# First loads as float32 on hardware queues, and batch 0's swapped x normed from its raw copy

## The chip, the cores and the metric

The kernel runs on one core of a Trainium2 chip. The metric is the device time of a whole execution in microseconds (us). A profile is one of these executions; its span is some 2 us shorter than the time. The profile calls the engines PE (TensorE), PEld (its weight loads), DVE (VectorE), ACT (ScalarE), POOL (GpSimd) and SP (SyncE).

## The reference, cut to what matters

```python
# 8 batches, 12 heads, 448 positions, head size 64
scores = scale * q @ k.T
attn = np.maximum(scores, 0.0) ** 2 / S
x = (attn @ v) in token order            # 3584 tokens, 768 features
rms = np.sqrt(np.mean(x * x, axis=-1, keepdims=True) + 1e-06)
xn = x / rms * rms_g
g = xn @ w_gate ; val = xn @ w_val       # 768 -> 1536
out = (silu(g) * val) @ w_out            # 1536 -> 768
```

## The kernel before: the parts that matter

The kernel handles one batch after the other. While PE multiplies batch b by the gate and value weights, pieces of the attention of batch b+1 are woven in. Batch 0 has no predecessor: its attention runs first, with nothing to hide behind. Three things are needed for what follows.

First, the loads. All of q, k and v come through the software queue (issued by POOL), which casts float32 to bf16 on the way:

```python
load("q", 0, 0, 2);  load("k", 0, 0, 2)      # first pair of heads
... # identity, constants, warm-up tile
load("q", 0, 2, 6);  load("k", 0, 2, 6)      # four heads in one load
load("v", 0, 0, 6)
load("q", 0, 6, 12); load("k", 0, 6, 12); load("v", 0, 6, 12)
for s in range(2): fetch_gv(s)               # first slices of the weights
alloc_ld(1)                                  # then q and k of batch 1, halves
```

Second, two layouts of x. A gate block multiplies 64 rows of x by gate weights and the other 64 rows by value weights at the same time, so each x is kept twice: `xT`, and `xD` with its two halves of 64 partitions swapped. `xD` is made by DMA (`swap`):

```python
def swap(b, j0, j1, eng=None):
    for hf in (0, 1):
        (eng or nc.sync).dma_start(out=xDs[b][own half, j0:j1, :], in_=xTs[b][other half, j0:j1, :])
```

Third, the order after the attention of batch 0. Three early blocks (`psE`) use the raw, not yet normed x and are scaled later; from the fourth block on (`psG`, `psV`) the normed x is used:

```python
rounds(0, 0, blocks[0], 0, KT, raw_x)      # early block 0, half that needs xT
norm_stat(0)                               # sums of squares on PE, root on ACT, reciprocal on DVE
rounds(0, 1, blocks[1], 0, KT, raw_x)
... # early blocks: first the part of raw xD that has landed
norm_apply(0)                              # six products on DVE into a new xT, swapped into a new xD by DMA
... # rest of raw xD, early block 2, then blocks 3 to 11 with normed xT and xD
```

`warm(n)` puts n dummy matmuls (`psW`) on PE to keep its clock up.

## Time and profile before

| | before |
|---|---|
| time, median of 4 fast runs | 463.41 us (463.32 to 463.87) |
| span of the profiled run | 461.8 us |
| PE busy | 97% |
| from 68 to 100 us, PE busy | 30.73 of 32 us |

PE is the bound from about 64 us on. What can be won lies before that. The lines below are from the page of the kernel before: busy time by engine, and the granted TensorE clock in 40 slices of the span, in tenths of full speed.

```profile
span 461.8 us, 10803 instructions
PE 445.7 (97%) x4718; PEld 249.4 (54%) x4718; DVE 268.2 (58%) x318; ACT 284.8 (62%) x425; POOL 53.6 (12%) x79
PEclk9799899999999999999999999999999999999999
```

Next, the table by stretches of the kernel before. The columns are: stretch; its length; busy us and instructions of PE, PEld, DVE, ACT and POOL; granted clock; mean DMA occupation; GB/s.

```profile
6.00:8.00 2.00, 0.55 (x4) 0.11 (x4) 0.42 (x1) 1.12 (x2) 2.00 (x4) 1.00 1.38 181
8.00:10.00 2.00, 0.56 (x17) 0.48 (x18) 0.00 (x0) 0.60 (x1) 2.00 (x4) 1.00 1.22 159
12.00:14.00 2.00, 2.00 (x16) 0.70 (x15) 2.00 (x3) 1.59 (x2) 0.70 (x1) 0.50 1.33 172
44.00:48.00 4.00, 3.95 (x26) 1.97 (x27) 3.24 (x6) 2.22 (x4) 0.70 (x1) 0.66 1.51 195
```

PE is hardly busy from 6 to 10 us, and then runs at half clock until 18 us (0.50 in the three stretches from 12 to 18); a second half-clock time falls into 44 to 49 us. The timeline of PE shows the waits; in brackets stands the idle time just before, and what ended it.

```profile
9.44 0.39 PE L134 MATMUL psT<-ident,kb 112*64 112x112 bf16 x8 [2.42 <-DMA kb<-in_k_dram]
36.08 1.42 PE L447 MATMUL psE<-xT,wgv_sb 64*128 64x448 bf16 x12
42.98 0.35 PE L447 MATMUL psE<-xD,wgv_sb 64*128 64x448 bf16 x1 [0.64 <-DMA xD<-xT]
44.02 0.72 PE L447 MATMUL psE<-xD,wgv_sb 64*128 64x448 bf16 x5 [0.69 <-DMA xD<-xT]
53.24 0.35 PE L447 MATMUL psG<-xD,wgv_sb 64*128 64x448 bf16 x1
54.14 0.35 PE L447 MATMUL psV<-xD,wgv_sb 64*128 64x448 bf16 x1 [0.56 <-DMA xD<-xT]
62.82 1.71 PE L263 MATMUL psAV<-r,vb 112*64 112x448 bf16 x16
```

The first wait is for K of the second head pair, the next two for the raw swaps, the fourth for the swap of the normed x. And this is the chain that ended last in the same kernel (start, us, what), from the statistics on:

```profile
37.49 1.27 PE psSS L380 x12
38.79 0.64 ACT rstd L389
39.45 2.96 DVE rstd L393
42.44 3.31 DVE xT L427 x6
46.28 7.82 DMA xD<-xT
54.14 0.35 PE psV L447
```

The chain does not run through PE's raw-swap waits or its half clock between 42 and 49 us at all: it runs through the norm and its swap. (0.9 us is the distance of the two starts at 53.24 and 54.14: a `psG` and a `psV` matmul run as a pair elsewhere, and here the second one came late. PE stood wholly idle for 0.56 us of it.)

### The profile page before, as it was taken

The page shows a single profiled execution, that of the slowest core. Times are in us where ns is not written, and L with a number is a line of the kernel's source. Part 1 is how long each engine was busy: PE and PEld are TensorE (multiplying, and loading weights), DVE is VectorE, ACT ScalarE, POOL GpSimd, SP SyncE. Part 2 cuts the span into 40 slices and gives each one's busy share as a digit, 9 for nine tenths or more (in the row PEclk, how much of TensorE's full clock was granted, in tenths as well). Part 3 has the DMA queues.
Part 4 walks back from the last instruction along what each step waited for, and adds up shares of the span by engine and source line. Part 5 has one row for each costly group of instructions (what it writes and reads, how often), then busy time and mean ns, then how long its engine had stood idle before and what let it go on. Part 6 is the DMA issues. An engine that isn't in the chain of part 4 may idle for free.

```text
span 461.8 us, 10803 instructions
## 1 busy us (share of the span) xinstructions
PE 445.7 (97%) x4718; PEld 249.4 (54%) x4718; DVE 268.2 (58%) x318; ACT 284.8 (62%) x425; POOL 53.6 (12%) x79
## 2 busy tenths in 40 slices
PE   5998989999999999999999999999999999999996
PEld 2334444665556555555556555565556555565664
DVE  2886776628664466477754466577754466552210
ACT  3696687637757667576757667586757567552221
POOL 8333220210000300003000200003000000000000
PEclk9799899999999999999999999999999999999999
DMA  9999999994401999039961999029930820032013
GB/s 108 191 206 206 208 206 175 187 203 114 88 1 35 208 180 138 2 80 192 176 77 25 208 178 134 16 75 208 179 64 18 190 82 1 1 95 70 1 35 104
DMA packets 86959, 53.89 MB, mean 117 GB/s; under 512 B 36608, under 2 KB 80512, under 8 KB 86912
## 3 DMA queue, kind: packets, MB, share of 16 engines
q0 software_dynamic: 44944, 27.73, 42.0%
q1 hardware_dynamic: 41712, 25.13, 27.2%
q8 instruction: 37, 0.61, 0.5%
q10 hardware_dynamic: 256, 0.34, 0.2%
q14 instruction: 10, 0.08, 0.1%
HBM read 47.19 MB, written 11.01 MB: 126 GB/s over the span
## 4 chain that ended last, share of the span: by engine, by line
PE 82%; DMA 5%; ACT 5%; DVE 4%; issue 1%; SPq 1%; POOL 1%; ACTq 0%; POOLq 0%
PE psG L447 34%; PE psO L380 19%; PE psAV L263 9%; PE psV L447 9%; PE psS L218 6%; DMA xD<-xT 4%; DVE xT L427 2%; PE psW L576 1%; DVE rstd L393 1%; PE psS L177 1%; DMA kb<-in_k_dram 1%; ACT r L207 1%; PE psT L134 1%; ACT sil L491 1%; ACT r L187 1%
## 5 line engine op out<-in xcount | busy, mean ns | idle before, releaser
L447 PEld LDWEIGHTS <-wgv_sb 64*128 64x128 bf16 x2304 | 123.4, 94 | 100.4 <-issue 14.9
L447 PE MATMUL psV<-xD,wgv_sb 64*128 64x448 bf16 x558 | 120.8, 349 | 1.7 <-DMA xD<-xT 1.7
L447 PE MATMUL psG<-xD,wgv_sb 64*128 64x448 bf16 x558 | 121.2, 349 | 0.0
L447 PE MATMUL psG<-xT,wgv_sb 64*128 64x448 bf16 x558 | 120.8, 350 | 0.0
L447 PE MATMUL psV<-xT,wgv_sb 64*128 64x448 bf16 x558 | 120.5, 350 | 0.1
L493 DVE TENSOR_TENSOR hT<-sil,psV 128x448 bf16<-128x448 bf16 x93 | 57.7, 620 | 107.9 <-ACT sil L491 106.9
L380 PE MATMUL psO<-wo_sb,hT 128*64 128x512 bf16 (+1 forms) x1344 | 113.5, 326 | 0.0
L232 ACT ACTIVATE r<-psS 112x896 bf16<-112x896 f32 x108 | 96.1, 917 | 22.8 <-PE psS L218 22.7
L380 PEld LDWEIGHTS <-hT 128*64 128x64 bf16 x1344 | 74.8, 110 | 36.3 <-issue 4.1
L491 ACT ACTIVATE sil<-psG 128x448 bf16<-128x448 f32 x93 | 50.6, 544 | 59.8 <-PE psV L447 38.9
L236 DVE TENSOR_TENSOR r<-r 112x1792 bf16<-112x1792 bf16 x72 | 78.4, 1089 | 4.9 <-ACT r L232 3.8
L513 ACT COPY ost<-psO 128x512 f32<-128x512 f32 (+1 forms) x54 | 25.1, 481 | 39.3 <-PE psO L380 35.0
L218 PE MATMUL psS<-qT,kT 64*128 64x448 bf16 (+1 forms) x288 | 47.8, 351 | 0.4 <-DVE r L230 0.4
L279 ACT ACTIVATE xT<-psAV,ga_sb 128x448 bf16<-128x448 f32 x48 | 28.1, 630 | 27.3 <-PE psAV L263 27.3
L263 PE MATMUL psAV<-r,vb 112*64 112x448 bf16 x384 | 42.3, 361 | 0.0
L230 DVE TENSOR_SCALAR r<-psS 112x896 bf16<-112x896 f32 x36 | 39.0, 1085 | 5.0 <-PE psS L218 5.0
L165 POOL DMA_DIRECT2D qT<-qT x12 | 6.5, 540 | 272.9 <-PE psS L218 139.0
L263 PEld LDWEIGHTS <-vb 112*64 112x64 bf16 x384 | 19.7, 110 | 20.5 <-issue 9.1
L218 PEld LDWEIGHTS <-kT 64*128 64x128 bf16 (+1 forms) x288 | 17.2, 97 | 19.3 <-issue 8.2
L427 DVE TENSOR_TENSOR xT<-xT,rstd 128x448 bf16<-128x448 bf16 x48 | 26.4, 619 | 0.3
L246 DVE TENSOR_TENSOR r<-r 112x1792 bf16<-112x1792 bf16 x23 | 24.6, 1086 | 2.2 <-ACT r L207 2.1
L187 ACT ACTIVATE r<-psS 112x896 bf16<-112x896 f32 x18 | 15.9, 919 | 12.0 <-PE psS L177 12.0
(61 smaller groups left out, 259.3 us busy)
## 6 DMA issues: line engine op xcount, KB each, us to landing
xD<-xT SPq DMA_DIRECT2D x32, 168.0 KB, 2.8
vb<-in_v_dram POOLq DMA_DIRECT2D x7, 672.0 KB, 19.2
qb<-in_q_dram POOLq DMA_DIRECT2D x6, 672.0 KB, 12.0
kb<-in_k_dram POOLq DMA_DIRECT2D x6, 672.0 KB, 14.5
qT<-qT POOLq DMA_DIRECT2D x24, 168.0 KB, 3.7
out_dram<-ost SPq DMA_DIRECT2D x7, 336.0 KB, 3.5
wgv_sb<-in_moe_w_gate_dram POOLq DMA_DIRECT2D x6, 384.0 KB, 16.4
wgv_sb<-in_moe_w_val_dram POOLq DMA_DIRECT2D x6, 384.0 KB, 17.1
```

The costliest lines, as they stand in the source:

```text
L218: nc.tensor.matmul(out=psS[: end - o, hf, :S], lhsT=flat[prt, o:end], rhs=qT[prt, 1 - hf : 3 - hf, h % HH], start=True, stop=True,)
L230: nc.vector.tensor_relu(out=r[:, cp], in_=src)
L232: nc.scalar.activation(out=r[:, cp], in_=src, func=ACT.Relu)
L236: nc.vector.tensor_tensor(out=r[:], in0=r[:], in1=r[:], op=ALU.mult)
L263: nc.tensor.matmul(out=part[hh * D : (hh + 1) * D, :], lhsT=ld["v", b][:, 2 * j + hh, c * D : (c + 1) * D], rhs=rsq[b, 2 * j + hh, c], sta ...
L279: nc.scalar.mul(out=xTs[b][:, j, :], in_=psAV[:, i, :], mul=ga_sb[:, j : j + 1])
L380: nc.tensor.matmul(out=ps[prt, :w], lhsT=lhsT[:, prt], rhs=rhs, start=start, stop=stop)
L427: nc.vector.tensor_tensor(out=xTs[b][:, kt, :], in0=src[:, kt, :], in1=rstds[b][:], op=ALU.mult)
L447: nc.tensor.matmul(out=parts[part][:, :S], lhsT=wgv_sb[prt, h, fb * P : (fb + 1) * P], rhs=src[prt, kt, :], start=(r == 0), stop=(r == 2 * ...
L491: nc.scalar.activation(out=s[:], in_=psG, func=ACT.Silu)
L493: nc.vector.tensor_tensor(out=hT[:, fb, o : o + S], in0=s[:], in1=psV, op=ALU.mult)
L513: nc.scalar.copy(out=ost[:, o : o + w], in_=ps[:, :w])
```

## The change

Its intent: let the attention of batch 0 start without a gap, and take the DMA swap out of the norm of batch 0. The diff, cut to its core:

```diff
-    load("q", 0, 0, 2)
-    load("k", 0, 0, 2)
+    for nm, src, eng in (("k", k, nc.sync), ("q", q, nc.scalar)):
+        first[nm] = fp.tile([PC, 2, NCH * D], FP32, ...)
+        eng.dma_start(out=first[nm][:], in_=head_rows(src, 0, 0, 2))
+    load("k", 0, 2, 4)
+    load("q", 0, 2, 4)
 ... # constants, identity; the warm-up tile's memset now first on DVE
+    nc.vector.tensor_copy(out=ld["k", 0][:, :2, :], in_=first["k"][:])
+    nc.scalar.copy(out=ld["q", 0][:, :2, :], in_=first["q"][:])
-    load("q", 0, 2, 6)
-    load("k", 0, 2, 6)
+    load("k", 0, 4, 6)
+    load("q", 0, 4, 6)
 ...
-            add(scores, j, (0, 1), (3,))
+            add(scores, j, (0, 1), (1,) if j == 0 else ())    # one relu of pair 0 to DVE
-            pair_scores(b, j, c, c == 3)
+            pair_scores(b, j, c, c == 3 and j > 0)            # one relu of batch 1 to ACT
 ...                                                           # leave: x of pair 5 by DVE, not ACT
-        rounds(0, 0, blocks[0], 0, KT, raw_x)
         norm_stat(0)
+        rounds(0, 0, blocks[0], 0, KT, raw_x)
 ...                                                           # norm_apply(0):
-        for kt in range(KT): xT = raw xT * rstd; swap(...)    # xD by DMA
+        for raw_x, x in zip((raw xT, raw xD), (xT, xD)):      # both by DVE
+            for kt in range(KT): x = raw_x * rstd
 ...                                                           # scaling of early blocks three units later
```

More of the change, by code (lines that the diff above doesn't have):

```diff
@@ L278, in leave @@
         for i, j in enumerate(js):
-            nc.scalar.mul(out=xTs[b][:, j, :], in_=psAV[:, i, :], mul=ga_sb[:, j : j + 1])
+            if b == 0 and j == HP - 1:
+                nc.vector.tensor_scalar_mul(
+                    out=xTs[b][:, j, :], in0=psAV[:, i, :], scalar1=ga_sb[:, j : j + 1]
+                )
+            else:
+                nc.scalar.mul(out=xTs[b][:, j, :], in_=psAV[:, i, :], mul=ga_sb[:, j : j + 1])
         nc.scalar.activation(
@@ L420, in norm_apply @@
     def norm_apply(b):
-        src = xTs[b]
+        raws = [xTs[b]]
         if b == 0:
+            raws.append(xDs[b])
             xTs[b] = npool.tile([P, KT, S], BF16, name="xT", tag="xT", bufs=2)
             xDs[b] = npool.tile([P, KT, S], BF16, name="xD", tag="xD", bufs=2)
-        for kt in range(KT):
-            nc.vector.tensor_tensor(
-                out=xTs[b][:, kt, :], in0=src[:, kt, :], in1=rstds[b][:], op=ALU.mult
-            )
-            if kt % 3 == 2:
-                swap(b, kt - 2, kt + 1)
+        for raw_x, x in zip(raws, (xTs[b], xDs[b])):
+            for kt in range(KT):
+                nc.vector.tensor_tensor(
+                    out=x[:, kt, :], in0=raw_x[:, kt, :], in1=rstds[b][:], op=ALU.mult
+                )
+                if b and kt % 3 == 2:
+                    swap(b, kt - 2, kt + 1)
     def hidden(b):
@@ L548 @@
     alloc_ld(0)
-    load("q", 0, 0, 2)
-    load("k", 0, 0, 2)
-    ident = const.tile([PC, PC], BF16, name="ident", tag="ident")
-    masks.make_identity(nc, ident[:])
-    ones_bf = const.tile([P, P], BF16, name="ones_bf", tag="ones_bf")
-    nc.vector.memset(ones_bf[:], 1.0)
-    eps_col = const.tile([P, 1], FP32, name="eps_col", tag="eps_col")
-    nc.vector.memset(eps_col[:], eps)
-    warm_act = const.tile([P, 1], FP32, name="warm_act", tag="warm_act")
-    nc.scalar.activation(out=warm_act[:], in_=eps_col[:], func=ACT.Sqrt)
@@ L559 @@
-    warm_in = const.tile([P, S], BF16, name="warm_in", tag="warm_in")
-    nc.vector.memset(warm_in[:], 0.0)
-    g_sb = wpool.tile([P, KT], FP32, name="g_sb", tag="rmsg")
-    nc.sync.dma_start(out=g_sb[:], in_=moe_rms_g.rearrange("(kt p) -> p kt", p=P))
+    first = {}
+    fpool = tc.tile_pool(name="first", bufs=1, side="right")
+    with fpool as fp:
+        for nm, src, eng in (("k", k, nc.sync), ("q", q, nc.scalar)):
+            first[nm] = fp.tile([PC, 2, NCH * D], FP32, name="first_" + nm, tag="first_" + nm)
+            eng.dma_start(out=first[nm][:], in_=head_rows(src, 0, 0, 2))
+        g_sb = wpool.tile([P, KT], FP32, name="g_sb", tag="rmsg")
+        nc.sync.dma_start(out=g_sb[:], in_=moe_rms_g.rearrange("(kt p) -> p kt", p=P))
+        load("k", 0, 2, 4)
+        load("q", 0, 2, 4)
+        ident = const.tile([PC, PC], BF16, name="ident", tag="ident")
+        masks.make_identity(nc, ident[:])
+        warm_in = const.tile([P, S], BF16, name="warm_in", tag="warm_in")
+        nc.vector.memset(warm_in[:], 0.0)
+        ones_bf = const.tile([P, P], BF16, name="ones_bf", tag="ones_bf")
+        nc.vector.memset(ones_bf[:], 1.0)
+        eps_col = const.tile([P, 1], FP32, name="eps_col", tag="eps_col")
+        nc.vector.memset(eps_col[:], eps)
+        warm_act = const.tile([P, 1], FP32, name="warm_act", tag="warm_act")
+        nc.scalar.activation(out=warm_act[:], in_=eps_col[:], func=ACT.Sqrt)
+        nc.vector.tensor_copy(out=ld["k", 0][:, :2, :], in_=first["k"][:])
+        nc.scalar.copy(out=ld["q", 0][:, :2, :], in_=first["q"][:])
@@ L563 @@
     ga_sb = wpool.tile([P, KT], FP32, name="ga_sb", tag="rmsga")
     nc.vector.tensor_scalar_mul(out=ga_sb[:], in0=g_sb[:], scalar1=inv_attn)
-    load("q", 0, 2, 6)
-    load("k", 0, 2, 6)
+    load("k", 0, 4, 6)
+    load("q", 0, 4, 6)
     load("v", 0, 0, 6)
+    load("k", 0, 6, 12)
     load("q", 0, 6, 12)
-    last_k = load("k", 0, 6, 12)
     load("v", 0, 6, 12)
@@ L618 @@
         near, far = KT + 4, 2 * KT
+        norm_stat(0)
         rounds(0, 0, blocks[0], 0, KT, raw_x)
-        norm_stat(0)
         rounds(0, 1, blocks[1], 0, KT, raw_x)
@@ L635 @@
         main = gate_value(0, EB)
-        sides = along(0.2, 1, [lambda fb=fb: early_scale(0, fb) for fb in range(EB)])
-        sides += along(2.2, 1, [lambda fb=fb: early_rest(0, fb) for fb in range(EB)])
+        sides = along(3.2, 1, [lambda fb=fb: early_scale(0, fb) for fb in range(EB)])
+        sides += along(5.2, 1, [lambda fb=fb: early_rest(0, fb) for fb in range(EB)])
         sides += along(0, (len(main) - 1) / len(steps), steps)
```

## The prediction

> What bounds the kernel now. The page of the kernel before shows TensorE (PE) busy 97% of a 461.8 us span, and the chain that ended last is 82% PE. From 68 to 100 us PE is busy 30.7 of 32 us (table by stretches), so only the first 64 us can give anything. There the timeline of PE and the chain of waits show three losses:
>
> 1. Start. The first pair's transposes begin at 5.16 us, when the 12 warm-up matmuls end; the second pair's wait 2.42 us for K and begin at 9.44, because heads 2 to 5 come in one load that lands 5.4 us after its issue at 4.01.
> 2. Clock. After that idle time the granted clock is 0.50 from 12 to 18 us. The Trainium skill, "TensorE: Matmul & The Clock Gate", Part 1, says that an idle window of about 3.4 us halves the clock; the trace agrees roughly (PE 0.55 us busy of 2 from 6 to 8, and again from 8 to 10). At half clock two pairs take 4.5 and 5.3 us between their qkT copies on VectorE; warm ones take 3.6 to 3.9, set by VectorE (0.62+1.09+2.08=3.8) and ScalarE (about 3.8).
> 3. Norm of batch 0. Statistics matmuls stand behind 1.35 us of early matmuls; then come root 0.64, reciprocal 2.95, six products 3.3, and a swap by DMA of 7.8 us landing at 54.1. PE waits only 0.9 us for it (53.24 to 54.14).
>
> What the change does. First pair: two float32 loads of 224 KB on hardware queues, beside software loads of the second pair, which are issued first (about 1.3 and 2.1 us). Bytes read from DRAM do not change. I estimate the first pair in by 4.3 us, plus a cast on each engine of about 0.5: ready when the warm-up ends, so pair 0 gains 0.2 us at most. The second pair lands at 5.5 to 6, its transposes follow at about 7.0 instead of 9.44, and PE should not fall to half clock, or for less time. VectorE takes one relu (1.09) of pair 0 and pays it back in batch 1. Compute alone would gain about 4 us by pair 3. Two loads hardly move and limit it: V heads 0 to 5 (landed about 13; needed now at 12.2) and K of batch 1 (landed 30.8; wanted at 33.8, now at 30.4). So I count 3.2 us.
>
> Norm: statistics first brings rstd 1.35 us earlier; six more products (3.3 us) replace the DMA, so normed xD is ready about 6 us earlier. Gain: only PE's 0.9 us. The waits for the raw swaps (0.64 and 0.69 us at 43 and 44 us) stay, as does the clock drop after them (0.66 from 44 to 48). VectorE gets 2.3 us more work where it is 84% busy; late hT products may cost PE 0.4 us.
>
> Sum: 3.2 + 0.9 - 0.4 = 3.7 us, all on the critical path, carried to the end: 459.6 us. Range 457.2 to 461.8. Chances: faster by over 2% 0.03, within 2% 0.96, slower 0.01.
>
> What the profile would show: second-pair transposes at 6.5 to 7.5 us; clock near 1 from 8 to 20; early matmuls (psE, psSS) starting at about 33 instead of 36.1; no PE wait on xD near 50; small waits of PE on V (about 12) or K of batch 1 (about 30); the same PE work after 64 us, shifted by 3.7.
>
> What would make it wrong: float32 loads landing after 6 us or holding up the second pair; the clock still halving (costs 2 us), or no longer halving after the raw swaps (gains 2); V or K of batch 1 later than now; VectorE backlog holding PSUM buffers after 50 us.

## The result and the profile after

The changed kernel takes 456.48 us (median of 4 fast runs, 455.86 to 457.02), the kernel before 463.41 us: 6.9 us less. The ratio is 0.9848, with a 95% interval of 0.9831 to 0.9865. (A ratio here is the mean time of one kernel's fast runs over that of the other's of the same rounds, so it is not quite the ratio of the medians quoted.) Executions over 1.5% slower than the fastest of the same kernel are left out of the means. The class forecast, within 2%, is right; the time lies below the range that was given, and the gain is nearly double the 3.7 us forecast.

The page of the changed kernel, the same lines as before:

```profile
span 454.8 us, 10811 instructions
PE 440.7 (97%) x4718; PEld 249.0 (55%) x4718; DVE 272.4 (60%) x326; ACT 285.2 (63%) x425; POOL 53.5 (12%) x79
PEclk9999999999999999999999999999999999999999
```

Its table by stretches, same columns:

```profile
6.00:8.00 2.00, 1.33 (x22) 0.66 (x22) 1.35 (x2) 0.92 (x1) 2.00 (x4) 1.00 1.11 124
12.00:14.00 2.00, 2.00 (x17) 0.80 (x16) 2.00 (x3) 0.80 (x2) 0.88 (x2) 1.00 1.42 187
44.00:48.00 4.00, 3.80 (x42) 1.93 (x37) 3.40 (x5) 3.25 (x5) 0.70 (x1) 1.00 1.66 187
```

Its timeline of PE:

```profile
7.16 0.39 PE L134 MATMUL psT<-ident,kb 112*64 112x112 bf16 x8
30.99 0.39 PE L134 MATMUL psT<-ident,kb 112*64 112x112 bf16 x8 [1.62 <-DMA kb<-in_k_dram]
33.14 1.32 PE L385 MATMUL psSS<-x,ones_bf 128*64 128x448 bf16 x12
39.43 0.72 PE L455 MATMUL psE<-xD,wgv_sb 64*128 64x448 bf16 x5 [0.32 <-DMA xD<-xT]
48.54 0.39 PE L134 MATMUL psT<-ident,kb 112*64 112x112 bf16 x8 [0.74 <-ACT sil L499]
55.35 1.70 PE L263 MATMUL psAV<-r,vb 112*64 112x448 bf16 x16
```

The second pair no longer waits; K of batch 1 now does, as forecast; the wait for the raw swaps has shrunk to 0.32 us; the wait for a normed xD is gone; the clock is never halved. The chain of waits of the changed kernel now goes through the raw swap and then through PE and ACT:

```profile
33.59 5.80 DMA xD<-xT
39.43 0.72 PE psE L455 x5
...
46.33 1.34 ACT r L207 x2
48.54 0.58 PE psT L134 x16
```

Its DVE timeline shows why the norm is off the path: both products are through at 44.67 us, and PE's first matmul with normed xD starts at 46.31.

```profile
38.16 3.30 DVE L435 TENSOR_TENSOR xT<-xT,rstd 128x448 bf16<-128x448 bf16 x6
41.38 3.29 DVE L435 TENSOR_TENSOR xD<-xD,rstd 128x448 bf16<-128x448 bf16 x6
```

Where the time went, from starts of PE's instructions in the two profiles:

| point | before | after | gained so far |
|---|---|---|---|
| second pair's transposes | 9.44 | 7.16 | 2.28 |
| first early or statistics matmul | 36.08 | 33.14 | 2.94 |
| first matmul of block 3 (`psG`) | 49.73 | 43.47 | 6.26 |
| transposes behind block 3 | 55.32 | 48.54 | 6.78 |
| attention values of batch 1, pair 0 | 62.82 | 55.35 | 7.47 |
| end of span | 461.8 | 454.8 | 7.0 |

The start gave 2.9 us, against 3.2 forecast. The other 4 us came between the first early or statistics matmul and the first values of batch 1. I call this the norm stage; its length is 26.74 us before and 22.21 us after, 4.5 us less, of which 0.5 us is lost again before the end. The forecast gave it 0.5 us. These are single profiles. In the profile of run e10 below, nearly the same kernel, PE does not wait for K of batch 1: there the start gave 3.7 us and the stage 3.2 us, so the K wait decides on which side of the border some of the gain is counted.

### The profile page after: what moved, and what is told of

The parts are those of the page before. It is cut to its first block, busy times and chain, and to the rows that moved or that the text cites. A ratio compares the mean times of both kernels' runs of the same rounds, so it can differ in the third digit from the quotient of the medians.

```text
span 454.8 us, 10811 instructions
## 1 busy us (share of the span) xinstructions
PE 440.7 (97%) x4718; PEld 249.0 (55%) x4718; DVE 272.4 (60%) x326; ACT 285.2 (63%) x425; POOL 53.5 (12%) x79
## 4 chain that ended last, share of the span: by engine, by line
PE 83%; DMA 8%; ACT 3%; DVE 2%; POOL 1%; issue 1%; SPq 0%; POOLq 0%
PE psG L455 36%; PE psO L385 22%; PE psV L455 8%; PE psAV L263 8%; PE psS L218 7%; DMA kb<-in_k_dram 6%; DMA xD<-xT 3%; ACT r L207 1%; DVE xT L435 1%; PE psS L197 1%; PE psE L455 1%; DVE rstd L398 1%; PE psSS L409 1%; PE psT L134 1%; ACT xT L284 1%
## 5 line engine op out<-in xcount | busy, mean ns | idle before, releaser
L232 ACT ACTIVATE r<-psS 112x896 bf16<-112x896 f32 x108 | 96.1, 917 | 22.7 <-PE psS L218 22.6
L285 ACT ACTIVATE x<-psAV 128x896 bf16<-128x896 f32 (+1 forms) x27 | 22.5, 835 | 2.2 <-DVE xT L280 2.2
## 6 DMA issues: line engine op xcount, KB each, us to landing
kb<-in_k_dram POOLq DMA_DIRECT2D x6, 672.0 KB, 15.3
```

What stands on the lines that cost most here:

```text
L232: nc.scalar.activation(out=r[:, cp], in_=src, func=ACT.Relu)
```

## The experiments

All twelve kernels gave correct results. All were timed in rounds with the kernel before, e1 to e4 on one chip, e5 to e8 on a second and e9 to e12 on a third. A profile is of one run, and not always of a typical one: those of e2, e3, e8, e9 and e10 are of the slowest of their four runs, those of e7 and e11 of the fastest.

| run | what it is | median us (range of 4) | ratio to before | clock of the 4 runs |
|---|---|---|---|---|
| e1_start_only | before + start part | 460.50 (459.59 to 462.02) | 0.993 | 0.990 to 0.995 |
| e2_norm_only | before + norm part | 460.51 (457.19 to 462.51) | 0.992 | 0.989 to 0.998 |
| e3_k1_early | after + earlier K of batch 1 | 456.38 (456.26 to 456.80) | 0.984 | 0.998 to 1.0 |
| e4_fed_swap | before + dummies in raw-swap wait | 463.38 (461.73 to 463.84) | 0.9984 | 0.991 to 0.996 |
| e5_norm_fed | norm part + dummies in first K wait | 457.99 (457.80 to 458.57) | 0.9882 | 0.998 to 1.0 |
| e6_soft_first | after, first pair by software queue | 457.59 (456.96 to 457.88) | 0.9868 | 0.998 to 1.0 |
| e7_swap_xd | after, normed xD by DMA | 457.95 (456.84 to 459.83) | 0.9882 | 0.995 to 1.0 |
| e8_stat_late | after, statistics in the old place | 456.12 (455.85 to 457.88) | 0.9846 | 0.999 to 1.0 |
| e9_before_fed | before + dummies in first K wait | 463.81 (461.36 to 464.29) | 1.0004 | 0.991 to 0.996 |
| e10_leave_act | after, last leave on ACT | 456.42 (455.95 to 457.07) | 0.9856 | 0.998 to 1.0 |
| e11_relu_back | after, relu of batch 1 on DVE | 456.38 (456.00 to 457.08) | 0.9859 | 0.998 to 1.0 |
| e12_combo | after + three small edits | 457.21 (454.82 to 457.33) | 0.986 | 0.998 to 1.0 |

The kernel before stood at 463.86 us beside e1 to e4, 464.04 beside e5 to e8, and 462.07 (fast runs alone) beside e9 to e12, where it scattered from 460.87 to 466.63 in fast runs (one more, 468.73, was slow). Against that last group small ratios mean little (the intervals reach 0.005 to 0.007 to each side, some 2.5 to 3 us), so e10 to e12 are judged against the 456.48 us of the changed kernel, which was not timed again beside them. Differences between groups below are of medians, and a few tenths of a us of them mean nothing.

### The two halves of the change, apart: e1 and e2

e1 takes from the change only the loads, casts and the relu of pair 0; e2 takes only the rest.

> The kernel before with only the start of the change (float32 first pair, order of loads, one relu of pair 0 on VectorE). Theory A (the surplus over the forecast comes from the raw-swap stage, and it comes because PE now waits for K of batch 1 between the last two leaves, so the last swap is not queued behind the one before it, the wait for it shrinks by about 1.0 us and the clock is not halved, 1.7 us): start 2.9 + 1.0 + 1.7 = 5.6 us less, about 457.8 us. Theory B (the surplus comes from the norm part of the change: statistics first, last leave on VectorE): only 2.9 us less, about 460.5 us, with the clock still at 0.5 for one window after the raw swaps.

> The kernel before with only the norm part of the change (statistics first, xD normed by VectorE, last leave on VectorE, one relu moved, scale steps later). Theory A: only the wait of 0.9 us for normed xD goes, about 462.4 us, the clock still halves after the raw swaps, PE still waits about 1.3 us for them. Theory B: 0.9 + 1.0 + 1.7 us less, about 459.8 us.

Both took 460.5 us in the median, 3.4 us less than before. By the medians the halves are worth the same, and add to about 6.7 us; e2's interval (0.9873 to 0.9967) leaves anything from 1.5 to 5.9 us. Neither theory fits: e1 has theory B's time, but its raw-swap waits shrank and its clock held after them, as in theory A (though without a K wait to bring it about), and e2 lies between the two with a wide scatter (its slowest run, the profiled one, has a clock of 0.989, its fastest, 457.19 us, one of 0.998). The timeline of PE in e1 shows what theory A left out:

```profile
32.39 1.42 PE L447 MATMUL psE<-xT,wgv_sb 64*128 64x448 bf16 x12
39.89 0.72 PE L447 MATMUL psE<-xD,wgv_sb 64*128 64x448 bf16 x5 [0.49 <-DMA xD<-xT]
47.50 0.35 PE L447 MATMUL psG<-xD,wgv_sb 64*128 64x448 bf16 x1 [0.56 <-DMA xD<-xT]
48.41 0.35 PE L447 MATMUL psV<-xD,wgv_sb 64*128 64x448 bf16 x1 [0.57 <-DMA xD<-xT]
49.39 0.35 PE L447 MATMUL psG<-xD,wgv_sb 64*128 64x448 bf16 x1 [0.26 <-DMA xD<-xT]
50.18 0.35 PE L447 MATMUL psV<-xD,wgv_sb 64*128 64x448 bf16 x1 [0.44 <-DMA xD<-xT]
60.30 1.70 PE L263 MATMUL psAV<-r,vb 112*64 112x448 bf16 x16
```

The early matmuls start 3.7 us sooner than before and the raw-swap waits are smaller, but then PE stands four times at the normed swap, and the clock is halved from about 51 to 54.5 us. The stage is 27.9 us long, longer than before. So the wait for the normed swap is no fixed 0.9 us: it grows when PE arrives sooner.

### Filling the raw-swap wait: e4

```diff
         norm_apply(0)
+        warm_s(7)          # seven dummy matmuls into a score buffer
         for fb in range(2): rounds(0, fb, blocks[fb], near, far, raw_x)
```

> The kernel before with seven dummy matmuls (about 1.7 us) put where PE waits for the raw swaps (42.3 to 44.0 us), all else the same. If the half clock from 45.3 to 48.7 us is caused by that idle time: clock 1.0 there and 1.7 us less, about 461.7 us. If the drop has another cause: no change, 463.4 us, or up to 0.4 us more.

The idle time did cause that clock drop in this sense: with it filled, the granted clock of the profiled run is 1.0 from 17 us on, and the mean clocks of the four runs are 0.991 to 0.996, against 0.985 to 0.991 in the kernel before beside them. But the time fell by only 0.5 us in the medians, and the interval of the ratio (0.9953 to 1.0014, so at most 2.2 us) includes no change. PE reached block 3 at 47.52 us instead of 49.73, and then waited for the normed swap:

```profile
51.31 0.35 PE L447 MATMUL psV<-xD,wgv_sb 64*128 64x448 bf16 x1 [0.35 <-DMA xD<-xT]
...
53.17 0.35 PE L447 MATMUL psV<-xD,wgv_sb 64*128 64x448 bf16 x1 [0.59 <-DMA xD<-xT]
```

So in the kernel before most of the half clock at 45 to 49 us cost nothing: it lay in the shadow of the norm chain. The stage became 0.57 us shorter by it in the profiles, not the 1.7 us expected.

### Filling the first K wait, without and with the norm part: e9 and e5

```diff
             if n % 3 == 2:
                 warm(2)
+            if n == 1:
+                warm(10)   # between the first scores and the second pair's transposes
```

> The kernel before with ten dummy matmuls in the 2.4 us in which PE waits for K of the second pair, and nothing else. Theory F (start and norm part are each worth little alone, because the normed swap of batch 0 then takes back what the start gives): no half clock before 20 us, early matmuls begin near 34 us instead of 36.1, but PE then waits 1 to 2 us more for the normed swap: 461.5 to 463 us. Theory of the forecast (the terms simply add): start worth about 1.9 us of the 3.2, so at most 461.5 us, and with what run e5 showed against e2 rather 460 us.

> The norm part of the change on the kernel before, with the old loads, and ten dummy matmuls in the 2.4 us in which PE waits for K of the second pair. Theory C (the start's worth is mostly that PE has no idle stretch, so the clock is not halved for two windows; the earlier data itself is worth under 1 us): no half clock before 20 us, and about 457 to 458 us in every run (the one run of the norm-only kernel that kept a clock of 0.998 took 457.19). Theory D (the start's worth is the earlier data, 2.9 us or more): at least 459.5 us.

These two kernels differ only by the norm part, and by nothing at the start. e9 gained nothing that can be measured (463.81 us, above the 461.5 to 463 us of theory F; ratio 1.0004, with a wide interval of 0.9942 to 1.0066), e5 gained 6.0 us. In e9 the early matmuls start at 34.49 us (36.08 before) and block 3 at 44.94 (49.73 before), 4.8 us ahead. Then this follows, in its timeline of PE and its table by stretches:

```profile
48.72 0.35 PE L447 MATMUL psG<-xD,wgv_sb 64*128 64x448 bf16 x1 [0.77 <-DMA xD<-xT]
49.65 0.35 PE L447 MATMUL psV<-xD,wgv_sb 64*128 64x448 bf16 x1 [0.59 <-DMA xD<-xT]
50.88 0.35 PE L447 MATMUL psG<-xD,wgv_sb 64*128 64x448 bf16 x1 [0.51 <-DMA xD<-xT]
52.08 0.53 PE L447 MATMUL psV<-xD,wgv_sb 64*128 64x448 bf16 x1 [0.85 <-DMA xD<-xT]
63.02 1.71 PE L263 MATMUL psAV<-r,vb 112*64 112x448 bf16 x16
```

```profile
52.00:53.00 1.00, 0.92 (x6) 0.44 (x6) 0.00 (x0) 0.00 (x0) 0.16 (x1) 0.50 1.45 197
```

PE waits 2.7 us in four pieces, and a half clock from 51 to 58 us follows (in e5, without these waits, there is none). The lead is gone at 63.02 us (62.82 before). In e5 there is no swap to wait for, and the lead stays.

e5 against the changed kernel says what the earlier data is worth by itself. With the old loads and only dummies in the gap, the time is 457.99 us, 1.5 us more than the changed kernel and 2.5 us less than e2, in whose profile the gap is open and the clock is halved from 10.9 to 17.7 us. So of the 4.0 us that the start part is worth on top of the norm part (460.51 to 456.48), about 2.5 us can be had by keeping PE busy, and about 1.5 us is the data. This split is rough: e2's four runs spread over 5.3 us, and the one with a clock of 0.998 took 457.19 us, less than any run of e5. Theory C had under 1 us for the data, so it is right in kind and a little off in size.

### Parts of the start: e6

```diff
-        for nm, src, eng in (("k", k, nc.sync), ("q", q, nc.scalar)): ... float32 tiles
+        load("k", 0, 0, 2); load("q", 0, 0, 2)
-        nc.vector.tensor_copy(...); nc.scalar.copy(...)
```

> The changed kernel with the first pair loaded by the software queue with cast, as before, ahead of the second pair; no float32 tiles and no cast instructions. If the float32 loads on the hardware queues matter: the second pair lands about 1.5 us later (two more issues of 0.7 us ahead of it), second-pair transposes near 8.5 us, 457.0 to 458.5 us. If only the splitting of heads 2 to 5 into pairs matters: same as the changed kernel, 456.4 us.

It took 457.59 us, 1.1 us more than the changed kernel and inside the range for "the float32 loads matter". The delay did not show where I expected it: the second pair was in time, but PE then waited 0.34 us for V and 0.97 us for the q of heads 6 to 11. The two extra issues on the software queue push back all that follow: the first load of V is issued at 5.91 us, at 4.61 in the changed kernel. The ranges of the two kernels just touch (456.96 us is e6's fastest run, 457.02 the slowest of the changed kernel), so the 1.1 us is rough.

### Parts of the norm: e7, e8, e10, e11

e7 goes back to the DMA swap for the normed xD only, with statistics still first; e8 puts the statistics back in their old place; e10 puts the last leave back on ACT; e11 puts the relu of batch 1 back on DVE.

> The changed kernel with the normed xD made by DMA swap again; statistics stay first. Theory E (the normed swap is the gate of the whole stage: it lands about 15 us after the statistics end, whatever PE does, and PE's own losses only hid it): swap lands near 49.5 to 50.5 us where PE wants it at 46.3, PE waits 2 to 4 us, perhaps with a halved clock after: 458.5 to 461 us. Theory of the forecast (its removal is worth the 0.9 us of PE's wait): 457.3 us.

> The changed kernel with the statistics matmuls behind the first early block again. Normed xD then comes 1.3 us later, near 46.0 us, just when PE wants it (46.3): 456.4 to 456.8 us if statistics first is worth little by itself; 457.7 us if the 1.35 us are on the critical path.

e7 took 457.95 us, 1.5 us more than the changed kernel, in runs from 456.84 to 459.83 whose clocks range from 1.0 to 0.995. The profiled run is the fastest of the four and has a full clock; the swap is on its chain of waits again, and the transfer lands at 47.95 us:

```profile
40.62 7.33 DMA xD<-xT
47.99 0.35 PE psV L453
```

The expected 458.5 to 461 us was too high; the 457.3 us of the forecast lies 0.65 us below the median, and inside the scatter. So with statistics first and no gap at the start, the swap alone costs about 1.5 us in the medians; the full-clock run lies within the range of the changed kernel, so the cost shows in the other three runs, with clocks of 0.995 to 0.998, which have no profile. e8 took 456.12 us: statistics first is worth nothing while xD is normed by DVE. Without either (e1) the kernel is 4.0 us slower, so either one seems to do most of the work. For statistics first this is not quite shown: e7 and e1 also differ by the moved leave and relu, which e10 and e11 undo only where DVE norms xD, and by the scaling of the early blocks three units later, which no run undoes alone.

> The changed kernel with the last leave (x of pair 5) on ScalarE again. In the changed kernel ScalarE's square waits for VectorE's product anyway (2.2 us, ended by VectorE), so I expect no difference: 456.2 to 456.9 us. If the VectorE leave sent the last raw swap off earlier: 457 us or more.

> The changed kernel with the relu of batch 1, pair 0, last chunk on VectorE again. VectorE is taken from 38.2 to 46.7 us by the products and squares, and that relu would stand behind the products at about 44.6 us, holding a score buffer: PE waits 1 to 3 us for it near 43 us, 457.5 to 459 us. If ScalarE's extra relu (it delays a Silu for which PE waits 0.74 us at 48.5) is the worse of the two: 455.8 us.

e10 (456.42 us) and e11 (456.38 us, not the 457.5 to 459 us expected) equal the changed kernel. In e11 PE does wait for the relu on DVE, but for 0.21 us only, and its wait for the Silu stays at 0.73 us, so the moved relu is not what delays that Silu. Both moves could be left out.

### Can the K wait be taken away? e3 and e12

```diff
+    load("q", 1, 0, HH); load("k", 1, 0, HH)      # both: ahead of fetch_gv(0), fetch_gv(1)
-        add(swap, 5, HP)
+        add(swap, 5, HP, (nc.sync, nc.scalar))    # e12 only
-        warm(12)
+        warm(10)                                  # e12 only
```

> The changed kernel with the first-half loads of q and k of batch 1 issued ahead of the first weight slices, so that PE's wait of 1.62 us for K near 30 us should go. Theory A: the last two swaps are again close together, PE waits about 1.0 us longer for the last one, and the clock may halve again (1.7): between 455.9 and 457.6 us, so little or no gain. Theory B: the 1.6 us are simply gained, about 454.9 us.

> The changed kernel with three small edits: loads of q and k of batch 1 ahead of the first weight slices, the last raw swap split over the SyncE and ScalarE queues, ten warm-up matmuls in place of twelve. The K wait near 30 us and most of the wait for the raw swaps should go and the start move up by at most 0.4 us: 455.2 to 456.0 us if those waits are on the path; 456.4 us as before if the swap's transfer time itself is the limit.

In e3 the K wait is gone, and PE waits 0.94 us in three pieces for the raw swaps instead of 0.32 us; the time is the same, as theory A said. e10 happens to show the same: its load of K came in time in the profiled run, and its timeline of PE has

```profile
38.58 0.35 PE L455 MATMUL psE<-xD,wgv_sb 64*128 64x448 bf16 x1 [0.40 <-DMA xD<-xT]
39.13 0.35 PE L455 MATMUL psE<-xD,wgv_sb 64*128 64x448 bf16 x1 [0.20 <-DMA xD<-xT]
40.03 0.72 PE L455 MATMUL psE<-xD,wgv_sb 64*128 64x448 bf16 x5 [0.56 <-DMA xD<-xT]
55.95 1.70 PE L263 MATMUL psAV<-r,vb 112*64 112x448 bf16 x16
```

So a wait for K and the waits for the raw swaps largely stand in for each other. e12 was to improve on the changed kernel and did not (457.21 us, not 455.2 to 456.0; one of four runs had 454.82). Its clean-up of waits bought nothing measurable.

### The norm stage in all profiles

From the first early or statistics matmul to the first values of batch 1 (`psAV`), one profile each. The K wait stands just before the stage, the raw-swap waits in it (both in us, 0 where the timeline lists none):

| kernel | normed xD by | K wait | starts | ends | length | raw-swap waits | half clock inside |
|---|---|---|---|---|---|---|---|
| before | DMA | 0 | 36.08 | 62.82 | 26.74 | 1.33 | 45.3 to 48.7 |
| e4 (with 7 dummies) | DMA | 0 | 35.68 | 61.85 | 26.17 | 0 | none |
| e1 | DMA | 0 | 32.39 | 60.30 | 27.91 | 0.67 | 51.1 to 54.5 |
| e9 | DMA | 0 | 34.49 | 63.02 | 28.53 | 0.17 | 51.2 to 58.1 |
| e7 (statistics first) | DMA | 0 | 31.76 | 55.99 | 24.23 | 0.43 | none |
| e2 | DVE | 0 | 36.21 | 61.46 | 25.25 | 1.18 | 45.0 to 48.4 |
| e8 (statistics late) | DVE | 1.20 | 32.85 | 55.18 | 22.33 | 0 | none |
| e5 | DVE | 0.67 | 34.93 | 57.18 | 22.25 | 0.30 | none |
| after | DVE | 1.62 | 33.14 | 55.35 | 22.21 | 0.32 | none |
| e6 | DVE | 0.45 | 34.09 | 56.87 | 22.78 | 0.74 | none |
| e12 | DVE | 0 | 32.98 | 55.89 | 22.91 | 0.33 | none |
| e11 | DVE | 0.56 | 32.23 | 55.24 | 23.01 | 0.59 | none |
| e3 | DVE | 0 | 32.26 | 55.59 | 23.33 | 0.94 | none |
| e10 | DVE | 0 | 32.40 | 55.95 | 23.55 | 1.16 | none |

With xD by DVE and a full clock the length is 22.2 to 23.6 us, wherever the stage starts, and 21.9 to 22.6 us without the raw-swap waits. With the swap and no statistics first it is 26.2 to 28.5 us, and longer in the two kernels where it starts well earlier (e1, e9). e2 is 3.0 us longer than e5; half of its 3.4 us at half clock explains 1.7 us of that, and its raw-swap waits of 1.18 us most of the rest.

## Why the prediction was wrong, point by point

- The start. "So I count 3.2 us." The profile shows 2.94 us at the first early matmul, and e1 alone gained 3.4 us. The second pair's transposes (7.16 us), the full clock from 8 to 20 us, the start at "about 33" (33.14) and a wait for K of batch 1 near 30 us came as said. V did not delay PE: POOL's next load, released by V in both kernels, was issued at 11.46 us instead of 13.30, so V had landed before the values were wanted at 12.49.
- The norm. "Gain: only PE's 0.9 us" is the step that failed. Together with the 0.4 us off for late hT products it made a term of 0.5 us. Measured, the norm part is worth 3.4 us alone (e2), 4.0 us on top of the start (e1 to the changed kernel) and 5.8 us on top of the filled gap (e9 to e5). I had taken a wait that was left over at the end of a chain for the worth of that chain. PE's other losses in the stage, 1.33 us of raw-swap waits and about 1.7 us of half clock (half of 3.4 us), ran beside the norm chain. With the swap in place, taking them away only lengthens the wait for it: e4 and e9 show it. In the two profiles 1.0 us less of raw-swap waits, 1.7 us of half clock and the 0.9 us make 3.6 of the 4.5 us that the stage lost; the rest is not traced.
- "The waits for the raw swaps ... stay, as does the clock drop after them." In the profile of the changed kernel the waits fell from 1.33 to 0.32 us and the drop went. The waits are not gone for good, though: where PE does not wait for K, they are 1.16 us (e10) and 0.94 us (e3). Part of this is SP's queue: one issue of the swap before the last took 1.48 us before and 1.46 us after, but in the changed kernel the K wait lies between the last two leaves, and that issue was over (32.48 us) before the last swap could start (33.09); before, the last swap had to queue behind it (37.10 us, while its x was ready at 35.95). In e9 and e5 all these issues took under 0.61 us, and the waits were 0.17 and 0.30 us. So this differs between profiles of kernels that issue the same swaps, and is not the doing of the change; its cause is open. No fast run of the changed kernel had a clock below 0.999; the kernel before had 0.985 to 0.996 in its fast runs beside the experiments. Why the drop went also where the waits stayed (e10) is not shown.
- "Sum: 3.2 + 0.9 - 0.4." Adding was not far off as arithmetic: the halves alone gave 3.4 and 3.4 us and the whole 6.9. It was the second number that was wrong. Adding does fail for smaller pieces: a filled start gap is worth nothing measurable without the norm part (e9) and about 2.5 us with it (e2 to e5, by medians).
- The list of what could go wrong named the right thing, a clock "no longer halving after the raw swaps (gains 2)", and the range left no room for it.

What stays open is when an idle time halves the clock. In the profile before, 1.33 us of waits in two pieces was followed by a half clock; in e2 1.18 us was, in e10 1.16 us in three pieces was not, and in the changed kernel 1.62 us in one piece near 30 us was not. The Trainium skill, "TensorE: Matmul & The Clock Gate", Part 1, has the activity watched in windows of 3413 ns that run free of the kernel. The profile before agrees with this: its clock changes at about 11.17, 18.00, 45.31 and 48.72 us (worked out from its mean clock in stretches of half a us, as 0.67 from 11.0 to 11.5), and the distances are 2, 8 and 1 times 3.41 us. So chance would decide where an idle time falls in the windows; that e2's four runs, the same kernel, had clocks from 0.989 to 0.998 fits this. No run here settles how much idle time in one window is too much.

## What to carry to other kernels

The idle time of the bound engine at the end of a side chain is not the worth of that chain. Compare the chain's end with when the engine would arrive if its own losses were gone; here the norm chain took 15.3 us from the end of the statistics (38.8 us) to the landing (54.1 us), and PE, without its losses, wanted its result some 5 us sooner (e9 reached block 3 4.8 us ahead). Two fixes that shadow each other must be tried together: each of the small repairs (dummies in the gap, dummies in the swap wait) did nothing measurable alone, and the first was worth about 2.5 us, by medians, once the chain was short. And a gap on TensorE can be filled with dummy matmuls where data cannot come sooner: by medians that gave 2.5 of the 4.0 us that the new loads gave.

## What the Trainium skill lacked or had wrong

- "TensorE: Matmul & The Clock Gate", Part 1, says in its table of states that the clock falls to half after at least one idle window of about 3.4 us. Here it fell after windows that were idle only in part: after waits of 1.33 us (before) and 1.18 us (e2), for 3.4 us each time. (Further on the page tells of a kernel in which frequent short idles did it too, but gives no amount.) The free-running window of 3413 ns itself agrees with the distances above.
- The same page gives N ÷ 1.2 GHz from start to start while cold; for 448 columns that is an estimate of 0.373 us. Weight loads of the first warm-up matmuls before are 0.37 us apart (2.03, 2.40, 2.78 us), which agrees; but the profile lists a granted clock of 1.00 in that time. No page says that the recorded clock reads full before its first change.
- "DMA: Bandwidth & Descriptors", section "Anatomy of one DMA — SWDGE (gpsimd) path", fits a DMA as 2.0 us plus bytes over 436 GB/s. For a software load of 224 KB of float32 (112 KB as bf16) that is an estimate of about 2.5 us; the first two in the kernel before, with least else in flight, took 3.2 and 2.9 us from issue to landing; the four small ones in the changed kernel a median of 4.2 us (K) and 4.3 us (q), with other loads in flight. The fit has no term for other loads in flight; whether they made the difference, no run shows.
- No page says that the issue of a DMA on SP's queue can take 0.6 or 1.5 us for the same transfer: 0.6 us in e9 and 1.48 us before.
